# A fused forward and backward pass on one core: keeping grad_out and half of a large tensor on chip between the stages, recomputing a factor instead of spilling it, and spreading one stage's tiles between another's matmuls

## The chip, the cores and the metric

The kernel runs on one core of a Trainium2 chip. A core has a matrix engine (TensorE, PE in the profile), a vector engine (VectorE, DVE), an activation engine (ScalarE, ACT), a general-purpose engine (GpSimd, POOL) and a queueing engine (SyncE, SP), each with its own instruction stream, and 16 DMA engines that move data between memory, the on-chip SBUF and PSUM, where the matmuls accumulate. The metric is the device time in microseconds of one execution of the whole kernel; lower is better.

## The reference

Given x (2048 x 640), wqkv (640 x 1920), wo (640 x 640), w1 (640 x 1728), w2 (1728 x 640), a gate vector and grad_out (2048 x 640), all bfloat16, the kernel computes the output of a gated mix of linear attention and a two-layer network, and the gradients of that output with respect to x, wqkv, wo, w1, w2 and the gate (seven outputs):

```python
qkv = (x @ wqkv).reshape(B, S, 3, H, Dh)             # H = 32 heads of Dh = 20
phi = lambda t: where(t > 0, t + 1, exp(t)) + 1e-6
pq, pk = phi(q), phi(k)
kv  = einsum("bhsd,bhse->bhde", pk, v);  z = einsum("bhsd->bhd", pk)
o   = einsum("bhqd,bhde->bhqe", pq, kv) / (einsum("bhqd,bhd->bhq", pq, z)[..., None] + 1e-6)
a   = o.reshape(B, S, D) @ wo
b   = relu(x @ w1) @ w2
g   = sigmoid((x * gate_w).sum(-1, keepdims=True))
out = g * a + (1 - g) * b
_, vjp = jax.vjp(f, x, wqkv, wo, w1, w2, gate_w);  grads = vjp(grad_out)
```

## The kernel before

The 2048 rows are cut into NT = 16 tiles of 128 rows. D = 640 gives KD = 5 column blocks, F = 1728 gives KF = 14 (the last one half filled). Groups of G = 4 row tiles share a buffer in several places. Everything is bfloat16 but the sums in PSUM and a few per-row vectors.

The stages, in order: the k stage (x transposed, pk = phi(k)); Y = x^T pk; the forward loop; dw2; X; the backward network stage with small matrix products between its tiles; dk and dw1; dwk and dwq; dx.

**Forward loop** (lines 558 to 573). For each row tile, `q_main` computes q and pq = phi(q) (name pq, tiles tb). `q_post` sums pq times z per head, adds 1e-6, multiplies by 1 + exp(-logit), and takes the reciprocal: grd, one number per row and head, the gate over the attention's denominator. GpSimd multiplies pq by it (L486): pqg. `load_T` sends pqg through a DMA transpose to pqT. Then the factor e = grd * min(pq - 1e-6, 1), the derivative of phi times grd, is made by one VectorE and one GpSimd operation (L490, L491). `q_store` writes each pair of tiles of pqg and of e to memory (pqg_d, e_d) and loads the pair's rows of grad_out into a ring do_r. `h_half` computes the hidden layer; `out_chunk`, two tiles later, the output from hT and pqT and the sum T_t of output times grad_out (L540).

**dw2 stage** (lines 616 to 656). PE's main work is hs^T times doX: 14 chunks w2p, each of 16 pairs of matmuls, one pair per row tile. doX is grad_out with H = 32 further columns; all of it is loaded in four pieces at the end of the forward loop (L573). Between the chunks stand the 16 r tiles. `r_main` multiplies doT (grad_out transposed, by DMA, one group of four tiles at a time) by MT into a PSUM tile rp, copies it to SBUF on ScalarE (L589), multiplies by pqg (L591), sums by head (L592), scales (L594), and has GpSimd make wz = z times the result (L596). `r_post` subtracts wz from rp (L604, which frees rp's PSUM buffer) and multiplies by e (L607) into dq_st, and `r_store` sends pairs of dq to memory. The subtraction of a tile is issued after the next tile's `r_main`. pqg comes back from memory in four loads, e in eight, three of them ahead. After chunks 2 to 12 one or two r tiles follow:

```python
while 1 < m and done < NT and done < (m - 1) * NT / (KF - 4):
    r_main(done)
    if done >= 1:
        r_post(done - 1)
```

After chunk 9 the four transposes of w2 (w2T) are issued on SP's queue.

**X stage** (L665): pqg^T times doX, five PSUM tiles xp. It ends with `load_T(KV2_s, KVT_d)`, whose result `small_0` (tiles dwo) uses two row tiles into the next stage, where XT, the transpose of X, and woT are loaded too.

**What sets the order.** The tile framework decides the order of the instructions on each engine's stream from the program order and from its own estimates, and puts in the waits. All PSUM tiles come from one pool of four buffers, used in turn. Nearly all of SBUF is one arena: the `_Arena` class is told each buffer's size and the time span in which it lives (model times T_FF, T_DW2 and so on), and places them so that buffers whose spans overlap don't share space; a buffer's first write waits until the earlier users of its space are done. Loads and transposes are issued by SP in stream order; most output stores by ScalarE.

Of the kernel before, what the change touches and what calls it, by code (L numbers as in the profile page):

```python
# [14 lines left out]
P = 128  # L15
H = 32
# [3 lines left out]
class _Arena:  # L20
# [9 lines left out]

    def plan(self, limit, trials=6000):
        import random
        rnd = random.Random(1)
        order = sorted(self.items.items(), key=lambda kv: -kv[1][0] * (kv[1][2] - kv[1][1]))
        best = self._plan_order(order)
        for _ in range(trials):
            if best <= limit:
                break
            new = order[:]
            for _ in range(rnd.choice((1, 1, 2, 3))):  # L40
                new.insert(rnd.randrange(len(new)), new.pop(rnd.randrange(len(new))))
            tot = self._plan_order(new)
            if tot <= best:
                best, order = tot, new
        return self._plan_order(order)

# [31 lines left out]
def kernel(  # L78
# [38 lines left out]
    TF = (T_DW2 - T_FF) / NT  # L117
    T_H = T_DW2 - 10
    ar.add("xN", NT * D * B2, 0, T_FF)
    for g in range(NG):  # L120
# [15 lines left out]
    ar.add("MT", KD * D * B2, T_FF, T_X)  # L136
    ring("pqst", 2 * D, 3, T_FF, T_DW2)
    ring("hTf", KF * P, 3, T_FF, T_DW2 + 10)
    ring("pqT", D, 4, T_FF, T_DW2 + 10)
    ring("est", 2 * D, 2, T_FF, T_DW2)  # L140
    ring("dor", 2 * D, 3, T_FF, T_DW2 + 10)
    ring("ost", 2 * D, 2, T_FF, T_DW2 + 15)
    ar.add("doX", NT * DX * B2, T_H, T_FB)
    ar.add("pqg", NT * D * B2, T_DW2 + 5, T_FB)
    for g in range(NG):
        ar.add(f"doT{g}", G * P * KD * B2, T_DW2 + 10 + 6 * g, T_FB + 12 + 30 * (g + 1))
    ring("er", 2 * D, 3, T_DW2 + 10, T_X)
    ring("dqst", 2 * D, 2, T_DW2 + 10, T_X)
# [76 lines left out]
    wqT_s, wkT_s = mat("wqT"), mat("wkT")  # L225
    pqgN = aview("pqg", NT * D, i=NT)
    doX = aview("doX", NT * DX, i=NT)
    dkg = [aview(f"dk{g}", G * D, i=G) for g in range(NG)]
# [15 lines left out]
    KVT_d = dram.tile([D, D], BF16, name="KVT_d")  # L244
    e_d = dram.tile([S, D], BF16, name="e_d")
    dq_d = dram.tile([S, D], BF16, name="dq_d")
# [228 lines left out]
    def q_post(i):  # L475
        pq, tz = pqs.pop(i)
        pr, ii = i // 2, i % 2
        grd = tmp("grd", 3, [P, H], FP32)
        nc.vector.tensor_reduce(grd[:], heads(tz[:]), AX.X, ALU.add)
        nc.vector.tensor_scalar(grd[:], grd[:], 1e-6, rg_t[:, i:i + 1], ALU.add, ALU.mult)  # L480
        nc.vector.reciprocal(grd[:], grd[:])
        if ii == 0:
            e_st[pr] = rnext("est").rearrange("p (i d) -> p i d", i=2)
            pq_st[pr] = rnext("pqst").rearrange("p (i d) -> p i d", i=2)
        pqg = pq_st[pr][:, ii, :]
        nc.gpsimd.tensor_tensor(heads(pqg), heads(pq[:]), hb(grd[:]), ALU.mult)  # L486
        pqTs[i] = rnext("pqT").rearrange("p (c s) -> p c s", s=P)
        load_T(pqTs[i], pqg)
        dph = tmp("tb", 8)
        nc.vector.tensor_scalar(dph[:], pq[:], -1e-6, 1.0, ALU.add, ALU.min)  # L490
        nc.gpsimd.tensor_tensor(heads(e_st[pr][:, ii, :]), heads(dph[:]), hb(grd[:]), ALU.mult)  # L491

    def q_store(pr):
        nc.sync.dma_start(rows2(pqg_d, pr), pq_st.pop(pr))
        nc.sync.dma_start(rows2(e_d, pr), e_st.pop(pr))
        do_r[pr] = rnext("dor").rearrange("p (i d) -> p i d", i=2)
        load_N(do_r[pr], do2[2 * pr * P:(2 * pr + 2) * P, :])

# [24 lines left out]
    def out_chunk(i):  # L523
        pr, ii = i // 2, i % 2
        hT, pqT = hTs.pop(i), pqTs.pop(i)
        if ii == 0:
            ops[i] = pp("op")
        op = ops.pop(i)
        for kf in range(KF - 1):
            mm_cols(op, hT[:, kf, :], lambda a, e: w2_s[:, kf, a:e], ii == 0 and kf == 0, False)  # L530
        for k in range(KD):
            mm_cols(op, pqT[:, k, :], lambda a, e: M_s[:, k, a:e], False, ii == 1 and k == KD - 1)
        if ii == 0:
            ops[i + 1] = pp("op")
            tail_pair(op, ops[i + 1], hT[:, KF - 1, :], hTs[i + 1][:, KF - 1, :], w2_s[:, KF - 1, :], True)
        if ii == 0:
            o_st[pr] = rnext("ost").rearrange("p (i d) -> p i d", i=2)
        nc.scalar.copy(o_st[pr][:, ii, :], flat(op)[:, 0:D])
        jk = tmp("tb", 8)
        nc.vector.scalar_tensor_tensor(jk[:], flat(op)[:, 0:D], 1.0, do_r[pr][:, ii, :], ALU.mult, ALU.mult,  # L540
                                       accum_out=T_t[:, i:i + 1])
        if ii == 1:
            nc.scalar.dma_start(rows2(o0, pr), o_st.pop(pr))
# [37 lines left out]

    rps = {}

    def r_main(i):
# [5 lines left out]
        t_ = tmp("tb", 8)  # L590
        nc.vector.tensor_tensor(t_[:], rb[:], pqgN[:, i, :], ALU.mult)  # L591
        nc.vector.tensor_reduce(u_all[:, i, :], heads(t_[:]), AX.X, ALU.add)  # L592
# [3 lines left out]
        nc.gpsimd.tensor_tensor(heads(wz[:]), heads(zb[:]), hb(w32[:]), ALU.mult)  # L596
        nc.scalar.copy(doX[:, i, D:DX], w32[:])
        rps[i] = rp, wz

    def r_post(i):  # L600
# [4 lines left out]
        if ii == 0:  # L605
            dq_st[pr] = rnext("dqst").rearrange("p (i d) -> p i d", i=2)
        nc.vector.tensor_tensor(dq_st[pr][:, ii, :], s_[:], e_r[pr][:, ii, :], ALU.mult)  # L607
        if ii == 1:
            e_r.pop(pr)
            if pr + 3 < NT // 2:  # L610
                e_load(pr + 3)

    def r_store(pr):
        nc.sync.dma_start(rows2(dq_d, pr), dq_st.pop(pr))
# [317 lines left out]
```

## Time and profile before

| what | value |
|---|---|
| time, median of 3 runs (lowest to highest) | 655.67 us (655.65 to 656.07) |
| the profiled execution: time / span in the trace | 655.64 us / 653.9 us |
| mean granted clock of TensorE | 0.995 |
| PE busy | 636.0 us (97%) |
| VectorE, ScalarE, GpSimd busy | 262.6, 150.8, 120.7 us |
| moved by DMA | 108.44 MB |
| forward loop's steady part, 80 to 220 us | PE busy 139.11 of 140 us |
| dw2 stage, 220 to 245, 245 to 275, 275 to 315 us | PE busy 21.56, 28.54, 39.69 us |

How to read the lines that follow. Times are in microseconds from the span's start. A line of the timeline gives start, duration, engine, source line, operation, written tile <- read tiles, the shape, and in brackets the idle time before it with what ended it. In a wait line the three numbers are the total, the count and the longest. A line of the windows gives the stretch and its length, the busy time of PE, weight loads, VectorE, ScalarE and GpSimd (instructions in brackets), the granted clock, the DMA engines' share and GB/s. "SPq" and "ACTq" are DMA issues on those engines' queues; "arena" is any buffer of the arena.

### The profile page before, as it was taken

To read this page: it belongs to the slowest core of one execution; us is meant where nothing else is said; L and a number is where in the kernel's file an instruction comes from. 1 tells how busy PE (TensorE), PEld (TensorE's weight loads), DVE (VectorE), ACT (ScalarE), POOL (GpSimd) and SP (SyncE) were. 2 spreads that over 40 slices of the span, in tenths; PEclk is the share of its full clock that TensorE was granted. 3 is DMA by queue.
4 is the path that set the end of the run, shared out by engine and by line. 5 is a ranking of instruction groups with operands and counts; after the bars stand their busy time and mean duration, and the time that the engine had idled before them with its cause. 6 is when DMAs were issued, how large, how long until landed. Compare 5 with 4: busy or idle time off the path is not lost.

```text
span 653.9 us, 10503 instructions
## 1 busy us (share of the span) xinstructions
PE 636.0 (97%) x4400; PEld 357.6 (55%) x4480; DVE 262.6 (40%) x518; ACT 150.8 (23%) x209; POOL 120.7 (18%) x111
## 2 busy tenths in 40 slices
PE   9979999999999979999999999999999999999998
PEld 5536555555555545555555555555555555555554
DVE  4994654555445206566126332221016320104442
ACT  4401322212222113232134343442110111110000
POOL 5840534333343103243001000000000000000000
PEclk9979999999999999999999999999999999999999
DMA  9991884765447899731759999794118449991111
GB/s 259 313 368 60 208 169 88 157 132 145 116 88 173 252 279 214 201 111 61 176 124 214 233 259 248 146 267 124 39 47 196 117 106 278 259 219 58 42 42 43
DMA packets 229209, 108.44 MB, mean 166 GB/s; under 512 B 181802, under 2 KB 228458, under 8 KB 229162
## 3 DMA queue, kind: packets, MB, share of 16 engines
q1 hardware_dynamic: 217194, 93.02, 61.5%
q10 hardware_dynamic: 11968, 14.75, 6.6%
q8 instruction: 35, 0.57, 0.4%
q14 instruction: 12, 0.10, 0.0%
HBM read 31.54 MB, written 30.97 MB: 96 GB/s over the span
## 4 chain that ended last, share of the span: by engine, by line
PE 87%; DVE 4%; SPq 3%; DMA 3%; issue 1%; ACT 1%; POOL 0%; DVEq 0%; ACTq 0%; POOLq 0%
SPq L307 3%; DMA arena<-in_grad_out_dram 2%; DVE arena L362 2%; PE yp_531 L317 1%; PE w1p_4639 L773 1%; PE w1p_4770 L773 1%; PE w1p_5090 L773 1%; PE w1p_4867 L773 1%; PE w1p_4571 L773 1%; PE w1p_5283 L773 1%; PE w1p_5226 L773 1%; PE w1p_5158 L773 1%; PE w1p_5021 L773 1%; PE w1p_4702 L773 1%; PE op_2315 L317 1%
## 5 line engine op out<-in xcount | busy, mean ns | idle before, releaser
L317 PEld LDWEIGHTS <-arena 128*128 128x128 bf16 x2818 | 219.0, 98 | 179.6 <-issue 11.0
L773 PEld LDWEIGHTS <-arena 128*128 128x128 bf16 x320 | 30.8, 98 | 26.9 <-issue 0.5
L686 PEld LDWEIGHTS <-arena 128*128 128x128 bf16 x320 | 30.5, 98 | 26.7 <-issue 1.3
L504 PEld LDWEIGHTS <-arena 128*128 128x128 bf16 x320 | 30.4, 98 | 25.8
L406 POOL TENSOR_TENSOR arena<-arena 128x640 f32<-128x640 f32 x14 | 20.1, 1434 | 4.8 <-DVE arena L362 4.0
L757 DVE TENSOR_TENSOR tb_4845<-dkp_4834,dzb 128x640 bf16<-128x640 f32 x1 | 0.8, 825 | 41.5 <-PE dkp_4834 L317 41.5
L669 PEld LDWEIGHTS <-arena 128*128 128x128 bf16 x80 | 7.8, 98 | 9.6 <-issue 0.3
L861 PEld LDWEIGHTS <-arena 128*128 128x128 bf16 x80 | 7.8, 98 | 9.5
L874 DVE SCALAR_TENSOR_TENSOR f_5688<-gwb,dl_t,arena 128x640 f32<-128x640 bf16 x1 | 0.9, 885 | 28.4 <-DMA arena<-dxB_d 28.4
L339 PEld LDWEIGHTS <-arena 128*128 128x128 bf16 x140 | 7.9, 97 | 2.1 <-issue 1.0
L317 PE MATMUL yp_489<-arena 128*128 128x512 bf16 (+1 forms) x32 | 4.9, 308 | 4.0 <-DVE arena L362 4.0
L722 POOL MEMSET arena<- 128x3200 bf16 x1 | 2.8, 2764 | 31.2 <-DMA arena<-arena 31.2
L862 PEld LDWEIGHTS <-arena 128*128 128x128 bf16 x80 | 7.8, 98 | 0.0
L670 PEld LDWEIGHTS <-arena 128*128 128x128 bf16 x80 | 7.8, 98 | 0.0
L591 DVE TENSOR_TENSOR tb_2492<-tb_2490,arena 128x640 bf16<-128x640 bf16 x1 | 0.5, 492 | 16.8 <-ACT tb_2490 L589 16.8
L317 PE MATMUL yp_531<-arena 128*128 128x128 bf16 (+1 forms) x31 | 6.6, 387 | 0.1
L773 PE MATMUL w1p_4639<-arena 128*128 128x432 bf16 x32 | 6.0, 346 | 0.0
L773 PE MATMUL w1p_4770<-arena 128*128 128x432 bf16 x32 | 6.0, 346 | 0.0
L773 PE MATMUL w1p_4571<-arena 128*128 128x432 bf16 x32 | 6.0, 346 | 0.0
L773 PE MATMUL w1p_4867<-arena 128*128 128x432 bf16 x32 | 6.0, 346 | 0.0
L773 PE MATMUL w1p_5090<-arena 128*128 128x432 bf16 x32 | 6.0, 346 | 0.0
L773 PE MATMUL w1p_5226<-arena 128*128 128x432 bf16 x32 | 6.0, 346 | 0.0
(1065 smaller groups left out, 1217.9 us busy)
## 6 DMA issues: line engine op xcount, KB each, us to landing
out_dram<-arena ACTq DMA_DIRECT2D x28, 160.0 KB, 3.6
pk_d<-arena SPq DMA_DIRECT2D x4, 640.0 KB, 9.5
arena<-in_grad_out_dram SPq DMA_DIRECT2D x8, 320.0 KB, 4.5
pqg_d<-arena SPq DMA_DIRECT2D x8, 320.0 KB, 5.7
e_d<-arena SPq DMA_DIRECT2D x8, 320.0 KB, 3.9
out_dram<-arena ACTq DMA_DIRECT2D x8, 320.0 KB, 2.6
arena<-pqg_d SPq DMA_DIRECT2D x4, 640.0 KB, 4.6
arena<-in_grad_out_dram SPq DMA_DIRECT2D x4, 640.0 KB, 7.9
```

The source lines that it names most:

```text
L307: nc.sync.dma_start_transpose(dst, src.rearrange("s (c p) -> s c p", p=P))
L317: nc.tensor.matmul(ps_tile[:, b, 0:e - a], lhsT=lhsT, rhs=rhs_fn(a, e), start=start, stop=stop, **kw)
L339: nc.tensor.matmul(ps_tile[:, bank, a - 512 * bank:e - 512 * bank], lhsT=lhsT_fn(j), rhs=rhs_mat[:, j, a:e], start=bank not in seen, stop= ...
L362: nc.vector.scalar_tensor_tensor(dst, ps_flat, 1.0 + 1e-6, cp[:], ALU.add, ALU.max)
L406: nc.gpsimd.tensor_tensor(zacc, zacc, pkN[:, i, :], ALU.add)
L504: nc.tensor.matmul(hp[:, nb, 0:NBW], lhsT=xT(i, k), rhs=w1_s[:, k, blk * NBW:(blk + 1) * NBW], start=(k == 0), stop=(k == KD - 1))
L669: nc.tensor.matmul(xp[:, 0, :], lhsT=lhsT, rhs=doX[:, i, 0:512], start=(i == 0), stop=(i == NT - 1))
L670: nc.tensor.matmul(xp[:, 1, 0:DX - 512], lhsT=lhsT, rhs=doX[:, i, 512:DX], start=(i == 0), stop=(i == NT - 1))
L686: nc.tensor.matmul(gp[:, nb, 0:NBW], lhsT=doTg[i // G][:, k, gsl(i)], rhs=w2T_s[:, k, blk * NBW:(blk + 1) * NBW], start=(k == 0), stop=(k ...
L773: nc.tensor.matmul(wp[:, nb, 0:NBW], lhsT=xN2[:, i, csl(m)], rhs=hs(i)[:, blk * NBW:(blk + 1) * NBW], start=(i == 0), stop=(i == NT - 1))
L861: nc.tensor.matmul(wp[:, 0, :], lhsT=lhsT, rhs=dqN[:, i, 0:512], start=(i == 0), stop=(i == NT - 1))
L862: nc.tensor.matmul(wp[:, 1, 0:D + 1 - 512], lhsT=lhsT, rhs=dqN[:, i, 512:D + 1], start=(i == 0), stop=(i == NT - 1))
```

## The change

grad_out: each group of four tiles of doX is loaded once, in the forward loop (before tiles 1, 5, 9 and 13), serves the sum T_t there, and stays until the X stage; the ring do_r and its eight loads go. pqg: groups 2 and 3 are written by GpSimd straight into the buffers that the later stages read; groups 0 and 1 are stored and reloaded as before (NSP = 2). e: it is no longer made, stored and reloaded; grd is kept for all tiles, and `e_prep` computes min(pqg - 1e-6 grd, grd), the same factor, in the dw2 stage, by one GpSimd and one VectorE operation per tile, in three buffers. The r tiles come when the count of matmul pairs reaches 24 + 11.5 k, also within a chunk. Since the arena's content changes, its plan is made anew, with a longer search.

```diff
...
     T_Y, T_FF, T_DW2, T_X, T_FB, T_DW1, T_DWK, T_DX, T_END = 26, 48, 190, 273, 296, 432, 512, 556, 640
     TF = (T_DW2 - T_FF) / NT
     T_H = T_DW2 - 10
+    NSP = 2
     ar.add("xN", NT * D * B2, 0, T_FF)
     for g in range(NG):
         ar.add(f"xT{g}", G * D * B2, 0, T_FF + 5 + (T_H - T_FF - 5) * (g + 1) / NG)
...
     ar.add("KVT", KD * D * B2, T_FF - 20, T_FF + 30)
     ar.add("M", KD * D * B2, T_FF, T_DW2 + 10)
     ar.add("MT", KD * D * B2, T_FF, T_X)
-    ring("pqst", 2 * D, 3, T_FF, T_DW2)
+    ring("pqst", 2 * D, 3, T_FF, T_FF + TF * G * NSP + 5)
     ring("hTf", KF * P, 3, T_FF, T_DW2 + 10)
     ring("pqT", D, 4, T_FF, T_DW2 + 10)
-    ring("est", 2 * D, 2, T_FF, T_DW2)
-    ring("dor", 2 * D, 3, T_FF, T_DW2 + 10)
+    ar.add("grd", NT * H * 4, T_FF - 10, T_X)
     ring("ost", 2 * D, 2, T_FF, T_DW2 + 15)
-    ar.add("doX", NT * DX * B2, T_H, T_FB)
-    ar.add("pqg", NT * D * B2, T_DW2 + 5, T_FB)
+    for g in range(NG):
+        ar.add(f"doX{g}", G * DX * B2, T_FF + TF * G * g, T_FB)
+        ar.add(f"pqg{g}", G * D * B2, T_FF + TF * G * g if g >= NSP else T_DW2 + 5, T_FB)
     for g in range(NG):
         ar.add(f"doT{g}", G * P * KD * B2, T_DW2 + 10 + 6 * g, T_FB + 12 + 30 * (g + 1))
-    ring("er", 2 * D, 3, T_DW2 + 10, T_X)
     ring("dqst", 2 * D, 2, T_DW2 + 10, T_X)
     ring("w2st", D, 4, T_DW2, T_X + 5)
     ar.add("w2T", KD * F * B2, T_X - 30, T_DW1)
...
     X_s, XT_s, woT_s, wvT_s, KV2_s = mat("X"), mat("XT"), mat("woT"), mat("wvT"), mat("KV2")
     dKV_s, dKVT_s, Q_s, N_s = mat("dKV"), mat("dKVT"), mat("Q"), mat("N")
     wqT_s, wkT_s = mat("wqT"), mat("wkT")
-    pqgN = aview("pqg", NT * D, i=NT)
-    doX = aview("doX", NT * DX, i=NT)
+    pqgg = [aview(f"pqg{g}", G * D, i=G) for g in range(NG)]
+    doXg = [aview(f"doX{g}", G * DX, i=G) for g in range(NG)]
+    grd_all = aview("grd", NT * H * 2).bitcast(FP32).rearrange("p (i h) -> p i h", i=NT)
     dkg = [aview(f"dk{g}", G * D, i=G) for g in range(NG)]
     dqN = aview("dq", NT * DQX, i=NT)
     dxB = aview("dxB", NT * D, i=NT)
...
     def hs(i):
         return hsg[i // G][:, i % G, :]
+    def pqg(i):
+        return pqgg[i // G][:, i % G, :]
+
+    def doX(i):
+        return doXg[i // G][:, i % G, :]
+
     def gsl(i):
         return slice((i % G) * P, (i % G + 1) * P)
...
     def q_post(i):
         pq, tz = pqs.pop(i)
         pr, ii = i // 2, i % 2
-        grd = tmp("grd", 3, [P, H], FP32)
-        nc.vector.tensor_reduce(grd[:], heads(tz[:]), AX.X, ALU.add)
-        nc.vector.tensor_scalar(grd[:], grd[:], 1e-6, rg_t[:, i:i + 1], ALU.add, ALU.mult)
-        nc.vector.reciprocal(grd[:], grd[:])
-        if ii == 0:
-            e_st[pr] = rnext("est").rearrange("p (i d) -> p i d", i=2)
-            pq_st[pr] = rnext("pqst").rearrange("p (i d) -> p i d", i=2)
-        pqg = pq_st[pr][:, ii, :]
-        nc.gpsimd.tensor_tensor(heads(pqg), heads(pq[:]), hb(grd[:]), ALU.mult)
+        grd = grd_all[:, i, :]
+        nc.vector.tensor_reduce(grd, heads(tz[:]), AX.X, ALU.add)
+        nc.vector.tensor_scalar(grd, grd, 1e-6, rg_t[:, i:i + 1], ALU.add, ALU.mult)
+        nc.vector.reciprocal(grd, grd)
+        if i < NSP * G:
+            if ii == 0:
+                pq_st[pr] = rnext("pqst").rearrange("p (i d) -> p i d", i=2)
+            pg = pq_st[pr][:, ii, :]
+        else:
+            pg = pqg(i)
+        nc.gpsimd.tensor_tensor(heads(pg), heads(pq[:]), hb(grd), ALU.mult)
         pqTs[i] = rnext("pqT").rearrange("p (c s) -> p c s", s=P)
-        load_T(pqTs[i], pqg)
-        dph = tmp("tb", 8)
-        nc.vector.tensor_scalar(dph[:], pq[:], -1e-6, 1.0, ALU.add, ALU.min)
-        nc.gpsimd.tensor_tensor(heads(e_st[pr][:, ii, :]), heads(dph[:]), hb(grd[:]), ALU.mult)
+        load_T(pqTs[i], pg)
     def q_store(pr):
-        nc.sync.dma_start(rows2(pqg_d, pr), pq_st.pop(pr))
-        nc.sync.dma_start(rows2(e_d, pr), e_st.pop(pr))
-        do_r[pr] = rnext("dor").rearrange("p (i d) -> p i d", i=2)
-        load_N(do_r[pr], do2[2 * pr * P:(2 * pr + 2) * P, :])
+        if pr in pq_st:
+            nc.sync.dma_start(rows2(pqg_d, pr), pq_st.pop(pr))
     def h_half(i, half):
         hp = pp("hp")
...
             o_st[pr] = rnext("ost").rearrange("p (i d) -> p i d", i=2)
         nc.scalar.copy(o_st[pr][:, ii, :], flat(op)[:, 0:D])
         jk = tmp("tb", 8)
-        nc.vector.scalar_tensor_tensor(jk[:], flat(op)[:, 0:D], 1.0, do_r[pr][:, ii, :], ALU.mult, ALU.mult,
+        nc.vector.scalar_tensor_tensor(jk[:], flat(op)[:, 0:D], 1.0, doX(i)[:, 0:D], ALU.mult, ALU.mult,
                                        accum_out=T_t[:, i:i + 1])
         if ii == 1:
             nc.scalar.dma_start(rows2(o0, pr), o_st.pop(pr))
...
     q_post(0)
     LAG = 2
     for i in range(1, NT + LAG):
+        if i < NT and i % G == 1:
+            g = i // G
+            load_N(doXg[g][:, :, 0:D], do2[g * G * P:(g + 1) * G * P, :])
         if i < NT:
             q_main(i)
             h_half(i, 0)
...
             out_chunk(i - LAG)
         if i < NT - 1 and i % 2 == 1:
             h_half(i, 1)
-        if i == NT - 1:
-            for g in range(NG):
-                load_N(doX[:, g * G:(g + 1) * G, 0:D], do2[g * G * P:(g + 1) * G * P, :])
-
-
-    e_r, dq_st = {}, {}
-
-    def e_load(pr):
-        e_r[pr] = rnext("er").rearrange("p (i d) -> p i d", i=2)
-        load_N(e_r[pr], e_d[2 * pr * P:(2 * pr + 2) * P, :])
+
+    dq_st = {}
     rps = {}
+
+    es = {}
+
+    def e_prep(i):
+
+        es[i] = tmp("e", 3)
+        nc.gpsimd.tensor_tensor(heads(es[i][:]), heads(pqg(i)), hb(grd6[:, i, :]), ALU.subtract)
+        nc.vector.tensor_tensor(heads(es[i][:]), heads(es[i][:]), hb(grd_all[:, i, :]), ALU.min)
     def r_main(i):
         rp = pp("rp")
...
         rb = tmp("tb", 8)
         nc.scalar.copy(rb[:], flat(rp)[:, 0:D])
         t_ = tmp("tb", 8)
-        nc.vector.tensor_tensor(t_[:], rb[:], pqgN[:, i, :], ALU.mult)
+        nc.vector.tensor_tensor(t_[:], rb[:], pqg(i), ALU.mult)
         nc.vector.tensor_reduce(u_all[:, i, :], heads(t_[:]), AX.X, ALU.add)
         w32 = tmp("grd", 3, [P, H], FP32)
         nc.vector.tensor_scalar(w32[:], u_all[:, i, :], rg_t[:, i:i + 1], None, ALU.mult)
         wz = tmp("f32", 3, dt=FP32)
         nc.gpsimd.tensor_tensor(heads(wz[:]), heads(zb[:]), hb(w32[:]), ALU.mult)
-        nc.scalar.copy(doX[:, i, D:DX], w32[:])
+        nc.scalar.copy(doX(i)[:, D:DX], w32[:])
         rps[i] = rp, wz
+        if i + 1 < NT:
+            e_prep(i + 1)
     def r_post(i):
         pr, ii = i // 2, i % 2
...
         nc.vector.tensor_tensor(s_[:], flat(rp)[:, 0:D], wz[:], ALU.subtract)
         if ii == 0:
             dq_st[pr] = rnext("dqst").rearrange("p (i d) -> p i d", i=2)
-        nc.vector.tensor_tensor(dq_st[pr][:, ii, :], s_[:], e_r[pr][:, ii, :], ALU.mult)
-        if ii == 1:
-            e_r.pop(pr)
-            if pr + 3 < NT // 2:
-                e_load(pr + 3)
+        nc.vector.tensor_tensor(dq_st[pr][:, ii, :], s_[:], es.pop(i)[:], ALU.mult)
     def r_store(pr):
         nc.sync.dma_start(rows2(dq_d, pr), dq_st.pop(pr))
-    e_load(0)
-    e_load(1)
-    e_load(2)
+    grd6 = u_all
+    nc.vector.tensor_scalar(grd6[:], grd_all, 1e-6, None, ALU.mult)
     for g in range(NG):
-        load_N(pqgN[:, g * G:(g + 1) * G, :], pqg_d[g * G * P:(g + 1) * G * P, :])
         load_T(doTg[g], do2[g * G * P:(g + 1) * G * P, :])
+        if g < NSP:
+            load_N(pqgg[g], pqg_d[g * G * P:(g + 1) * G * P, :])
+    e_prep(0)
+    R0, RSTEP = 24, 11.5
     done = 0
-    for m in range(KF):
-        wp = pp("w2p")
-        st = rnext("w2st")
-        if m < KF - 1:
-            for i in range(NT):
-                mm_cols(wp, hs(i)[:, csl(m)], lambda a, e: doX[:, i, a:e], i == 0, i == NT - 1)
-            nc.scalar.copy(st, flat(wp)[:, 0:D])
-            nc.scalar.dma_start(out_5[m * P:(m + 1) * P, :], st)
-        else:
-            for i in range(0, NT, 2):
-                for b, (a, e) in enumerate(DSPL):
-                    for t in range(2):
-                        nc.tensor.matmul(wp[t * FT:(t + 1) * FT, b, 0:e - a], lhsT=hs(i + t)[:, m * P:F],
-                                         rhs=doX[:, i + t, a:e], start=(i == 0), stop=(i == NT - 2),
-                                         skip_group_check=True)
-            w2e = tmp("f32", 3, dt=FP32)
-            w2o = tmp("f32", 3, dt=FP32)
-            nc.scalar.copy(w2e[:], flat(wp)[:, 0:D])
-            nc.scalar.dma_start(w2o[0:FT, :], w2e[FT:P, :])
-            nc.gpsimd.tensor_tensor(st[0:FT, :], w2e[0:FT, :], w2o[0:FT, :], ALU.add)
-            nc.scalar.dma_start(out_5[m * P:F, :], st[0:FT, :])
-        while 1 < m and done < NT and done < (m - 1) * NT / (KF - 4):
+
+    def r_due(step):
+        nonlocal done
+        if done < NT and step >= R0 + RSTEP * done:
             r_main(done)
             if done >= 1:
                 r_post(done - 1)
...
             done += 1
             if done == NT:
                 r_post(NT - 1)
+
+    for m in range(KF):
+        wp = pp("w2p")
+        st = rnext("w2st")
+        if m < KF - 1:
+            for i in range(NT):
+                r_due(m * NT + i)
+                mm_cols(wp, hs(i)[:, csl(m)], lambda a, e: doX(i)[:, a:e], i == 0, i == NT - 1)
+            nc.scalar.copy(st, flat(wp)[:, 0:D])
+            nc.scalar.dma_start(out_5[m * P:(m + 1) * P, :], st)
+        else:
+            for i in range(0, NT, 2):
+                for b, (a, e) in enumerate(DSPL):
+                    for t in range(2):
+                        nc.tensor.matmul(wp[t * FT:(t + 1) * FT, b, 0:e - a], lhsT=hs(i + t)[:, m * P:F],
+                                         rhs=doX(i + t)[:, a:e], start=(i == 0), stop=(i == NT - 2),
+                                         skip_group_check=True)
+            w2e = tmp("f32", 3, dt=FP32)
+            w2o = tmp("f32", 3, dt=FP32)
+            nc.scalar.copy(w2e[:], flat(wp)[:, 0:D])
+            nc.scalar.dma_start(w2o[0:FT, :], w2e[FT:P, :])
+            nc.gpsimd.tensor_tensor(st[0:FT, :], w2e[0:FT, :], w2o[0:FT, :], ALU.add)
+            nc.scalar.dma_start(out_5[m * P:F, :], st[0:FT, :])
         if m == KF - 5:
             for q_ in range(4):
                 load_T(w2T_s[:, :, q_ * 432:(q_ + 1) * 432], B_w2[q_ * 432:(q_ + 1) * 432, :])
...
```

More of the change, by code (lines that the diff above doesn't have):

```diff
@@ L29, in add, with plan @@
         self.items[name] = [nbytes, t0, t1, None]
-    def plan(self, limit, trials=6000):
+    def plan(self, limit, seeds=24, trials=3000):
         import random
[L33 to L45, printed above, removed]
+        start = sorted(self.items.items(), key=lambda kv: -kv[1][0] * (kv[1][2] - kv[1][1]))
+        found = (self._plan_order(start), start)
+        for seed in range(seeds):
+            rnd = random.Random(seed)
+            order, best = start, self._plan_order(start)
+            for _ in range(trials):
+                if found[0] <= limit:
+                    break
+                new = order[:]
+                for _ in range(rnd.choice((1, 1, 2, 3))):
+                    new.insert(rnd.randrange(len(new)), new.pop(rnd.randrange(len(new))))
+                tot = self._plan_order(new)
+                if tot <= best:
+                    best, order = tot, new
+                    if best < found[0]:
+                        found = (best, order)
+        return self._plan_order(found[1])
     def _plan_order(self, order):
@@ L244 @@
     KVT_d = dram.tile([D, D], BF16, name="KVT_d")
-    e_d = dram.tile([S, D], BF16, name="e_d")
     dq_d = dram.tile([S, D], BF16, name="dq_d")
@@ L458 @@
     nc.vector.tensor_scalar(omg_t[:], g_t[:], -1.0, 1.0, ALU.mult, ALU.add)
-    e_st, pq_st, do_r, pqTs, hTs, o_st = {}, {}, {}, {}, {}, {}
+    pq_st, pqTs, hTs, o_st = {}, {}, {}, {}
     pqs = {}
@@ L667 @@
         for i in range(NT):
-            lhsT = pqgN[:, i, csl(m)]
-            nc.tensor.matmul(xp[:, 0, :], lhsT=lhsT, rhs=doX[:, i, 0:512], start=(i == 0), stop=(i == NT - 1))
-            nc.tensor.matmul(xp[:, 1, 0:DX - 512], lhsT=lhsT, rhs=doX[:, i, 512:DX], start=(i == 0), stop=(i == NT - 1))
+            lhsT = pqg(i)[:, csl(m)]
+            nc.tensor.matmul(xp[:, 0, :], lhsT=lhsT, rhs=doX(i)[:, 0:512], start=(i == 0), stop=(i == NT - 1))
+            nc.tensor.matmul(xp[:, 1, 0:DX - 512], lhsT=lhsT, rhs=doX(i)[:, 512:DX], start=(i == 0), stop=(i == NT - 1))
         nc.scalar.copy(X_s[:, m, :], flat(xp)[:, 0:D])
```

## The prediction

> **What bounds the kernel now.** I read the page's first line and busy times, then PE's waits, then the windows by stage, then PE, SP, DVE and POOL along the dw2 stage (220 to 312 us), where nearly all of the change lies.
>
> ```profile
> span 653.9 us, 10503 instructions
> PE 636.0 (97%) x4400; PEld 357.6 (55%) x4480; DVE 262.6 (40%) x518; ACT 150.8 (23%) x209; POOL 120.7 (18%) x111
> ...
> PE rp_2479 L317 <- DMA arena<-in_grad_out_dram: 3.3, 1, 3.3
> PE w2p_2814 L317 <- DVE tb_2750 L604: 1.2, 1, 1.2
> PE mtp_816 L339 <- DVE arena L510: 0.2, 1, 0.2
> 80.00:220.00 140.00, 139.11 (x929) 76.41 (x946) 68.91 (x137) 31.57 (x40) 55.45 (x43) 1.00 0.62 137
> 220.00:245.00 25.00, 21.56 (x158) 11.95 (x160) 1.84 (x5) 3.69 (x6) 0.72 (x1) 1.00 1.10 290
> ```
>
> PE is busy 636.0 of 653.9 us, and the change leaves its matmuls as they are. After 60 us PE waits 4.7 us in all; the two large waits stand in dw2: 3.28 us for doT0 (first r tile) and 1.25 us for an r tile's subtraction. So at most 4.5 us can be won, and the question is what new waits the denser r loop makes. The profiled execution took 655.64 us (1.74 outside the span) against a median of 655.67; I sum on 655.64. A difference of 0.2%, 1.31 us, is about what a measurement of this kernel can tell from none.
>
> **What costs nothing.** In the forward loop 16 POOL multiplies (1.27 us each, 20 us), 16 DVE operations, and the stores and loads of e and of half pqg go. There PE is 139.11 of 140 us busy and waits for nobody: no gain. The doX loads come earlier, under a DMA share of 0.62. They would cost only if a load held up SP's queue in which pqT and hT stand; at one place it does: hT15's transpose, issued at about 216.0 behind doT1, is wanted at 221.4, and with a transpose's 5.4 to 5.7 us (the KVT one below took 5.4) it is 0 to 0.3 late; I take 0.1. The first three e tiles and the DVE operation for 1e-6 times grd fall into 220 to 245, where DVE is busy 1.84 of 25 us and PE has two dw2 chunks before r0: nothing. If pqg0 landed later than 231, they would delay the first r product; it is issued at 217.6 and such loads take 4.6 to 7.7.
>
> **The first r tile.** Today doT0's transpose is issued at 230.83, behind the e loads and pqg loads, and lands 12.3 us later; the other doT transposes take 6.1 to 6.6 us. After the change SP's order is hT14, doT1, pqT15, hT15, pqg0, pqg1, doT2, w2T0, doT0. w2T0 reuses space of w2 and waits for the last output tile's matmuls (225.2), its issue takes 2.8 to 3.3; doT0 then goes out at about 228.2. PE wants r0 after 24 matmul pairs: w2 begins at 226.72, a chunk of 16 pairs takes 4.35, a pair 0.272, so 233.24. Landing after 5.4 (the KVT transpose) to 6.6 gives 233.6 to 234.8, a wait of 0.3 to 1.6; I take 1.0 for the 3.28.
>
> **The 1.25 us wait.** It came from a dq store issued late behind four w2T transposes:
>
> ```profile
> 251.51 13.19 SPq L307 DMA_TRANSPOSE arena<-in_B_w_dram  x4
> ...
> 265.37 0.47 SPq L614 DMA_DIRECT2D dq_d<-arena  x1
> ...
> 269.80 0.49 DVE L607 TENSOR_TENSOR arena<-tb_2725,arena 128x640 bf16<-128x640 bf16 x1 [1.37 <-DMA dq_d<-arena]
> ```
>
> These transposes now precede the first dq store, so the wait goes: -1.25.
>
> **The r loop.** An r tile comes every 11.5 pairs: T = 11.5 x 0.272 + 1.36 = 4.48 us. Each now also needs a POOL subtract (L591 of the new file) and a DVE minimum (L592). By the instruction order of the new program, DVE does for tile i: product (L601), subtraction of tile i-1 (L616), reduction, dq product of i-1 (L619), scale (L604), minimum for tile i+2. POOL does the subtract for tile i+2, then wz(i) (L606). The subtract has to wait until L619 of i-1 frees one of three e buffers; wz(i), queued behind it, waits too; and the subtraction of tile i waits for wz(i). That closes a cycle from one L616 to the next:
>
> ```profile
> 252.97 0.82 DVE L604 TENSOR_TENSOR tb_2580<-rp_2500,f_2518 128x640 bf16<-128x640 f32 x1
> 253.71 0.81 DVE L592 TENSOR_REDUCE u_all<-tb_2572 128x32 f32<-128x640 bf16 x1
> 254.43 0.48 DVE L607 TENSOR_TENSOR arena<-tb_2580,arena 128x640 bf16<-128x640 bf16 x1
> ...
> 69.08 1.27 POOL L491 TENSOR_TENSOR arena<-tb_842,grd_836 128x640 bf16<-128x640 bf16 x1
> 255.21 1.38 POOL L596 TENSOR_TENSOR f_2577<-zb,grd_2575 128x640 f32<-128x640 bf16 x1 [4.04 <-DVE grd_2575 L594]
> ```
>
> From the starts: subtraction 0.74, reduction 0.72, dq product 0.48, hand-over 0.08; then POOL 1.25 (like L491) and 1.36 (L596), hand-over 0.06: C = 4.69. Single terms vary (POOL 1.23 to 1.38, hand-over 0.08 to 0.16): 4.54 to 4.83. That is without a collision of minimum and wz, which become ready at the same moment. The minimum reads two SBUF tensors. The nearest rows are L442's products, also with two SBUF inputs, beside POOL's adds:
>
> ```profile
> 36.21 2.00 DVE L442 SCALAR_TENSOR_TENSOR tb_523<-arena,gwb 128x640 bf16<-128x640 bf16 x1
> 38.88 0.81 DVE L442 SCALAR_TENSOR_TENSOR tb_525<-arena,gwb 128x640 bf16<-128x640 bf16 x1
> 39.62 2.01 DVE L442 SCALAR_TENSOR_TENSOR tb_527<-arena,gwb 128x640 bf16<-128x640 bf16 x1
> ...
> 36.07 1.46 POOL L406 TENSOR_TENSOR arena<-arena 128x640 f32<-128x640 f32 x1
> 39.10 1.84 POOL L406 TENSOR_TENSOR arena<-arena 128x640 f32<-128x640 f32 x1 [1.57 <-DVE arena L362]
> ```
>
> L442 takes 0.81 alone and 2.0 when it starts in a POOL add, ending 0.68 after the add's end (38.21 after 37.53); the add in turn takes 1.84 instead of 1.46 when a product runs before it. So I take it that the two don't overlap: the minimum ends 0.62 after wz, and the product of the next tile (0.41), which stands behind it on DVE, still comes before L616: C = 0.74 + 0.72 + 0.48 + 0.08 + 1.25 + 1.27 + 0.62 + 0.41 = 5.57; if the minimum goes first, up to 5.8; down to 5.5 with the shorter hand-overs. Ends for the cycle: 4.54 to 5.8, value 5.57, since L442 is the nearest row in operands.
>
> The Trainium skill speaks against this step ("SBUF — State Buffer", "Who interferes with whom"): a VectorE instruction with two SBUF inputs and a GpSimd instruction that reads SBUF exclude each other, and the second one blocks fully until the first has ended. L442 beside L406 agrees. By that rule the sum below is 666.6; by the undisturbed durations of the operations alone it would be 655.2.
>
> What PE pays: PSUM's four buffers go round, and r15 needs the buffer of r13, which L616 frees. Measured from r0's start, the first L616 stands behind the product of r1: r1 starts at 12 x 0.272 + 1.36 = 4.62, copy and product take 2.69 (rp_2559 at 250.28, L604 at 252.97), the subtraction 0.82, hand-over 0.06: 8.2. Unhindered, r15 starts at 173 x 0.272 + 15 x 1.36 = 67.3. So the loss is 13 C - 59.1: 1.9 us at 4.69, nothing at 4.55, 3.7 at 4.83, 13.3 at 5.57 (12.4 at 5.5, 16.3 at 5.8). It shows at r4, r5, r8, r11, r12 and r15, at up to 3.4 us each.
>
> **KV2.** Its transpose went first after the X stage:
>
> ```profile
> 330.94 3.18 SPq L307 DMA_TRANSPOSE arena<-KVT_d  x1
> 334.24 5.17 SPq L307 DMA_TRANSPOSE arena<-arena  x4
> 339.58 3.41 SPq L307 DMA_TRANSPOSE arena<-in_A_wo_dram  x1
> ...
> 345.97 0.52 PE L339 MATMUL dwo_3569<-arena 128*128 128x140 bf16 x7
> ```
>
> Its new place in SBUF lies over the last pqg group, which the X stage reads to its end, and the scheduler puts it behind four XT transposes and woT. XT0 at 332.8, 4 x 1.33, woT 3.46: issue at 341.6, and with its 5.4 us it lands at 347.0; PE wants it at 345.97. Cost 0.8 to 2.0, taken 1.1.
>
> **Sum.** 655.64 - 3.28 - 1.25 + 1.0 + 0.1 + 1.1 = 653.3 without the loop; with its 13.3: 666.6. Own range 664 to 670 (cycle 5.5 to 5.8, other terms by their bounds).
>
> **Rivals.**
> - The loop keeps up (faster). If subtract and wz take their shorter times and the minimum doesn't block, the cycle is at most 4.55 and the time 653.3. Below a cycle of 4.62 the kernel is faster by over 1.31 us. For it: POOL is busy 9.54 of 30 us in dw2 now, DVE 16.91. Against it: L442's rows.
> - The loop lags by POOL's serial work alone: 4.69, loss 1.9, time 655.2; within 0.2% from 4.62 to 4.83. That is the case of the minimum not being held off although L442 is; its output is written over its input and one operand is a broadcast, which no row shows.
> - doT0 lands as late as it does now, 12.3 us after its issue, because doT2 and w2T0 crowd the DMA engines (share 1.10 in 220 to 245): r0 waits 7.3 instead of 1.0, 6.3 us more: 672.9 with the blocked minimum, 661 without. Against it: some 4 MB of transfers around it are gone.
> - The change doing less than it says: no case, the order shows the e traffic gone.
>
> **Numbers.** Forecast 0.66; keeps up 0.13 (faster); lags by POOL alone 0.12 (same); doT0 late 0.09 (slower). So faster 0.13, same 0.12, slower 0.75. The range takes in forecast and the third case, 654.5 to 670.5, and leaves out the faster rival and most of the late doT0, 0.19.
>
> **What would show it.** L592 at about 1.9 instead of 0.8, ending some 0.6 after L606; L616 every 5.6 us; PE waits for L616 at r4 to r15 adding up to 13; r0 waiting 1 for grad_out; the first dwo matmul 1.1 for KVT; no wait behind a dq store. I am wrong if L592 stays at 0.8 beside a running L606, or L616 keeps to 4.5.

## The result, and the profile after

The changed kernel takes 672.23 us (median, 671.61 to 673.42) against 655.87 for the kernel before in the same comparison: 1.025 times as long, 95% interval 1.0232 to 1.0268. The profiled execution took 672.27 us, span 670.2. The forecast was slower, 666.6 us, with a range up to 670.5; the sign and the main cause held, the size did not.

The head of the page after, and PE's waits (total, count, longest):

```profile
span 670.2 us, 10459 instructions
PE 639.3 (95%) x4400; PEld 358.3 (53%) x4480; DVE 283.8 (42%) x519; ACT 150.4 (22%) x209; POOL 118.8 (18%) x111
```

```profile
PE rp_2340 L327 <- DMA arena<-in_grad_out_dram: 4.5, 1, 4.5
...
PE rp_2758 L327 <- DVE tb_2729 L616: 3.1, 1, 3.1
PE rp_3131 L327 <- DVE tb_3101 L616: 2.8, 1, 2.8
PE rp_2916 L327 <- DVE tb_2886 L616: 2.8, 1, 2.8
PE dwo_3523 L349 <- DMA arena<-KVT_d: 1.4, 1, 1.4
...
PE rp_2547 L327 <- DVE tb_2518 L616: 1.1, 1, 1.1
PE rp_2973 L327 <- DVE tb_2940 L616: 1.0, 1, 1.0
PE rp_2601 L327 <- DVE tb_2571 L616: 0.7, 1, 0.7
```

The six tiles that wait for L616 are r8, r15, r11, r4, r12 and r5, the six that were named, for 11.5 us together. The wait behind a dq store is gone. Two things are larger than forecast: the first r tile waits 4.5 us for grad_out, and PE is busy 639.3 us instead of 636.0 with the same matmuls. The windows show where the second comes from (the third number from the end is the granted clock):

```profile
225.00:229.80 4.80, 4.80 (x38) 2.67 (x36) 4.47 (x4) 0.69 (x1) 3.33 (x3) 1.00 0.83 170
236.50:239.30 2.80, 2.65 (x11) 1.28 (x12) 0.00 (x0) 0.00 (x0) 0.00 (x0) 0.50 0.95 190
239.30:242.40 3.10, 3.10 (x19) 1.60 (x18) 1.55 (x3) 0.91 (x2) 0.33 (x1) 0.70 0.88 184
242.40:245.00 2.60, 2.55 (x20) 1.46 (x20) 0.00 (x0) 0.69 (x1) 0.94 (x1) 1.00 0.91 188
...
320.50:324.80 4.30, 4.30 (x24) 2.15 (x22) 3.25 (x7) 0.69 (x1) 1.53 (x2) 0.70 0.21 76
```

After the idle 4.5 us the clock is 0.50, then 0.70: r0 takes 2.63 us instead of 1.36 and the eight pairs after it 3.10 instead of 2.17, a loss of 2.2. Behind r15's wait it falls again; r15 and eleven pairs take 6.1 instead of 4.35, a loss of 1.8. In the kernel before, the wait of 3.28 us left it at 1.00.

The r loop in the profile after, first VectorE, then GpSimd:

```profile
246.16 0.82 DVE L616 TENSOR_TENSOR tb_2415<-rp_2340,f_2358 128x640 bf16<-128x640 f32 x1
...
247.62 0.48 DVE L619 TENSOR_TENSOR arena<-tb_2415,e_2285 128x640 bf16<-128x640 bf16 x1
...
249.48 1.87 DVE L592 TENSOR_TENSOR e_2461<-e_2461,arena 128x640 bf16<-128x640 bf16 x1 [1.23 <-POOL e_2461 L591]
251.28 0.48 DVE L601 TENSOR_TENSOR tb_2453<-tb_2451,arena 128x640 bf16<-128x640 bf16 x1
251.68 0.81 DVE L616 TENSOR_TENSOR tb_2464<-rp_2391,f_2409 128x640 bf16<-128x640 f32 x1
```

```profile
248.18 1.27 POOL L591 TENSOR_TENSOR e_2461<-arena,u_all 128x640 bf16<-128x640 bf16 x1 [4.84 <-DVE arena L619]
249.41 1.27 POOL L606 TENSOR_TENSOR f_2409<-zb,grd_2407 128x640 f32<-128x640 bf16 x1
```

L619 frees the e buffer, GpSimd subtracts, then makes wz; the minimum starts with wz (249.48 against 249.41) and ends at 251.35, 0.67 after it; the product and L616 follow. From one L616 to the next it is 5.52 us. The minimum is not slow by itself: where GpSimd was idle, in the same kernel, it took 0.81 (the second line here; in the first, GpSimd ran a subtraction from 226.48 to 228.33).

```profile
227.12 1.89 DVE L592 TENSOR_TENSOR e_2361<-e_2361,arena 128x640 bf16<-128x640 bf16 x1
228.94 0.81 DVE L592 TENSOR_TENSOR e_2412<-e_2412,arena 128x640 bf16<-128x640 bf16 x1
```

### The profile page after: what moved, and what is told of

Same layout as the page of the kernel before. It is cut to its first block, busy times and chain, and to the rows that moved or that the text cites. A ratio compares the mean times of both kernels' runs of the same rounds, so it can differ in the third digit from the quotient of the medians.

```text
span 670.2 us, 10459 instructions
## 1 busy us (share of the span) xinstructions
PE 639.3 (95%) x4400; PEld 358.3 (53%) x4480; DVE 283.8 (42%) x519; ACT 150.4 (22%) x209; POOL 118.8 (18%) x111
## 4 chain that ended last, share of the span: by engine, by line
PE 76%; DVE 5%; issue 4%; POOL 2%; DMA 2%; ACT 0%; ACTq 0%
DVE u_all L602 1%; DMA arena<-in_grad_out_dram 1%; PE w1p_4593 L788 1%; PE w1p_4724 L788 1%; DMA arena<-KVT_d 1%; PE w1p_5180 L788 1%; PE w1p_4975 L788 1%; PE w1p_4525 L788 1%; PE w1p_5044 L788 1%; PE w1p_4821 L788 1%; PE w1p_4656 L788 1%; PE w1p_5237 L788 1%; PE w1p_5112 L788 1%; PE op_2230 L327 1%; DVE arena L619 1%
## 5 line engine op out<-in xcount | busy, mean ns | idle before, releaser
L327 PE MATMUL yp_488<-arena 128*128 128x512 bf16 (+1 forms) x32 | 4.7, 299 | 4.0 <-DVE arena L372 4.0
L327 PE MATMUL rp_2340<-arena 128*128 128x512 bf16 (+1 forms) x10 | 2.8, 472 | 4.5 <-DMA arena<-in_grad_out_dram 4.5
```

The costliest lines, as they stand in the source:

```text
L327: nc.tensor.matmul(ps_tile[:, b, 0:e - a], lhsT=lhsT, rhs=rhs_fn(a, e), start=start, stop=stop, **kw)
```

## The experiments

The theory: the recomputed e makes the loop late, because VectorE operations with two SBUF inputs and GpSimd operations run one after the other; the late first r tile and the clock behind it come on top. Rivals: GpSimd's two operations in series are enough; the dense spacing of the r tiles is what cannot be kept; the loop's pace swallows the first tile's wait.

**The e work.** First, L592 left out, so that e lacks the minimum everywhere:

```diff
-        nc.vector.tensor_tensor(heads(es[i][:]), heads(es[i][:]), hb(grd_all[:, i, :]), ALU.min)
```

> The changed kernel without the minimum of e (L592): e is pqg - 1e-6 grd everywhere. Theory (operations of VectorE with two SBUF inputs and GpSimd's operations exclude each other): the minimum's 1.87 us go, but the next product (two SBUF inputs) now collides with GpSimd: the cycle becomes about 5.0 us, loop waits about 5 to 6 instead of 11.5, time near 667. Rival (only GpSimd's two operations in series matter, the minimum is slow by itself): cycle 4.7, the product stays at 0.48, loop waits 2, time near 663.

One execution, 661.05 us; r waits for L615 (the subtraction) 3.3 us, for grad_out 4.1. The cycle is 4.84 to 4.90, between the two expectations. The time lies under both (667 and 663): with waits of at most 1.2 us in the loop the slow matmuls behind r15, 1.8 us in the changed kernel, are gone too, and neither had counted them. The rows show the exclusion still at work, now on the product:

```profile
254.18 1.21 DVE L600 TENSOR_TENSOR tb<-tb,arena 128x640 bf16<-128x640 bf16 x1 [1.62 <-ACT tb L598]
258.52 0.49 DVE L600 TENSOR_TENSOR tb<-tb,arena 128x640 bf16<-128x640 bf16 x1 [1.13 <-ACT tb L598]
```

```profile
253.77 1.27 POOL L605 TENSOR_TENSOR f<-zb,grd 128x640 f32<-128x640 bf16 x1
258.62 1.53 POOL L605 TENSOR_TENSOR f<-zb,grd 128x640 f32<-128x640 bf16 x1
```

In the first pair the product is held until wz is nearly done (it ends at 255.39, wz at 255.04; 0.7 us added); in the second the product comes first and wz is 0.26 longer.

Then the subtract of e moved to VectorE, so that GpSimd has only wz:

```diff
-        nc.gpsimd.tensor_tensor(heads(es[i][:]), heads(pqg(i)), hb(grd6[:, i, :]), ALU.subtract)
+        nc.vector.tensor_tensor(heads(es[i][:]), heads(pqg(i)), hb(grd6[:, i, :]), ALU.subtract)
```

> The changed kernel with the subtract of e on VectorE instead of GpSimd: GpSimd has only wz in the loop, VectorE 4.0 us of own work per tile. Exclusion theory: wz (1.27) overlaps none of subtract, minimum and product, so the cycle is 4.0 + 1.27 = 5.2 us, some rows of L591, L592 or L601 are longer by up to 1.2 us, and the loop waits about 8 us: near 669. Rival (the queue on GpSimd makes the cycle): 4.5 us, no loop waits, about 661.

664.76 us, 1.0121 (1.0096 to 1.0145). The cycle is 4.95, not 4.5 as the rival wants: with GpSimd's queue out of the way the loop is still late, by 4.2 us of waits instead of 11.5.

```profile
252.64 0.81 DVE L591 TENSOR_TENSOR e<-arena,u_all 128x640 bf16<-128x640 bf16 x1
253.49 1.78 DVE L592 TENSOR_TENSOR e<-e,arena 128x640 bf16<-128x640 bf16 x1
```

```profile
252.87 1.72 POOL L606 TENSOR_TENSOR f<-zb,grd 128x640 f32<-128x640 bf16 x1 [3.24 <-DVE grd L604]
```

wz is held 0.45 by the subtract, then holds the minimum, which ends 0.68 after it: three operations in line. The expectation was 0.25 too long for the cycle and 4 us too long for the time.

Last, the part undone: e is made in the forward loop, stored, and reloaded in pairs, as in the kernel before; the rest stays changed.

```diff
+        nc.vector.tensor_scalar(dph[:], pq[:], -1e-6, 1.0, ALU.add, ALU.min)
...
+        nc.gpsimd.tensor_tensor(heads(ef[i][:]), heads(dph[:]), hb(grd), ALU.mult)
...
+            nc.sync.dma_start(e_d[j * P:(j + 1) * P, :], ef.pop(j)[:])
...
-        nc.gpsimd.tensor_tensor(heads(es[i][:]), heads(pqg(i)), hb(grd6[:, i, :]), ALU.subtract)
-        nc.vector.tensor_tensor(heads(es[i][:]), heads(es[i][:]), hb(grd_all[:, i, :]), ALU.min)
...
+            load_N(es[i // 2], e_d[i * P:(i + 2) * P, :])
```

> The changed kernel with one part undone: e is made in the forward loop, stored and reloaded (ring of four pairs); order of the r tiles and places in SBUF as in the changed kernel. Theory: all of the r loop's waits (11.5 us) go, since they come from the e work on GpSimd and VectorE; the first r tile waits as long as there or some 3 us longer, as two e loads go out ahead of doT0, with the lowered clock behind it: 661 to 664. Rival: the dense spacing of the r tiles itself makes the loop late; then half of its waits stay: 667 or more.

658.76 us, 1.0031 (1.0014 to 1.0047); span 657.3, 12.9 less than the changed kernel's. PE's waits in this run:

```profile
PE rp L333 <- DMA arena<-in_grad_out_dram: 4.8, 1, 4.8
PE yp L333 <- DVE arena L378: 4.0, 1, 4.0
PE warm L392 <- DVE arena L382: 1.3, 1, 1.3
PE dwo L355 <- DMA arena<-KVT_d: 1.2, 1, 1.2
```

No r tile waits for a subtraction any more, at the same spacing: the spacing alone does not make the loop late, the e work at this spacing does. No run has the e work at the old spacing. With the waits went r15's clock loss of 1.8 us, which the expectation had not counted; that is most of the 2 us by which the time lies under 661. The wait for doT0 was 0.3 us longer than in the changed kernel.

**The first r tile.** The r tiles of group 1 first, whose doT1 has landed long before:

```diff
+    seq = [4, 5, 6, 7, 0, 1, 2, 3] + list(range(8, NT))
...
-            r_main(done)
+            r_main(seq[done])
```

> The changed kernel, with the r tiles taken in another order: group 1 (tiles 4 to 7) first, then group 0, 2, 3. doT1 has landed long before r0 is due, so PE does not stop for grad_out. Theory: the wait of 4.5 us, and the lowered clock behind it (10 + 16 matmuls that took 2.2 us too long), are lost time that adds to the loop's, so the time falls by 6.7 us to about 665.5, with the r loop's waits as before (11 to 12 us, a subtraction every 5.5 us). Rival: the loop's pace absorbs an earlier start, or the clock drops at another place instead: then less than 3 us are won, 669 or more.

665.01 us, 1.013 (1.0102 to 1.0159); the span falls by 6.6 to 663.6. The wait for grad_out is gone, and what was won at r0 was not swallowed: r1 starts 4.7 us earlier than in the changed kernel, and so does r15. That the 6.6 come so near the expected 6.7 is in part luck. A new wait of 1.9 us stands before the first r tile, so that its start is only 2.5 us earlier (2.2 more are the clock there); the other 1.8 are r15's clock loss, which did not come this time, although its wait was 2.81 us again. Instead the clock fell to 0.66 in 275 to 280, behind r8's wait; these 1.5 us were swallowed, as the loop's waits fell from 11.5 to 10.1.

```profile
PE rp L327 <- DVE tb L616: 10.1, 6, 3.1
...
PE rp L327 <- DVE tb L547: 1.9, 1, 1.9
```

L547 is the last output tiles' sum, which frees a PSUM buffer and stands on VectorE behind the first three minimums, which wait for pqg1 here and run from 228.90 to 233.3. The prediction put these at nothing; in the changed kernel, where they needed pqg0 and ran from 225.3 to 229.7, that held.

The other side: the kernel before, with the spread of the r tiles alone.

```diff
-        while 1 < m and done < NT and done < (m - 1) * NT / (KF - 4):
...
+        if done < NT and step >= 24 + 11.5 * done:
```

> The kernel before with one part of the change alone: r tiles due every 11.5 matmul pairs from pair 24 on, everything else (e, pqg and doX from memory) as before. Theory: the spread needs doT0 at 233, and in the old traffic it lands at about 243, so TensorE stands 9 to 10 us instead of 3.3 and then runs at a lowered clock for some 2.5 us more; the r loop itself keeps up, since it has no e work. 664 to 668. Rival: the spread is what lets the r loop run without waits, and a late doT0 costs no more than it did: 652 to 656.

661.74 us, 1.0059 (1.0038 to 1.008).

```profile
PE rp L317 <- DMA arena<-in_grad_out_dram: 9.6, 1, 9.6
```

```profile
240.00:245.00 5.00, 2.93 (x11) 1.42 (x12) 0.00 (x0) 0.05 (x1) 0.00 (x0) 0.50 1.12 227
```

In the old traffic doT0 lands at 242, PE stands 9.6 us and comes back at half clock; no r tile waits for VectorE. The wait was as expected; the time came out 2 us below, and the dq store's wait of 1.25 us, which is gone here too, is a part of that. So the spread needs an early doT. In the changed kernel r0 starts 5.4 us earlier than here, and in e_spilled_alone, where e is still stored and reloaded, 4.0 us earlier; so most of this comes with the rest of the change, which keeps grad_out and half of pqg on chip. It was not early enough.

**The clock.** Five idle times of TensorE in each of two runs (one execution each), made by chains of VectorE copies between chunks of the dwk and dwq products of the kernel before:

```diff
+            nc.vector.tensor_copy(dm[:], flat(pv)[:, 0:D])
+            for _ in range(KS[m]):
+                nc.vector.tensor_copy(dm[:], dm[:])
+            nc.vector.tensor_copy(db[:], dm[:])
+            nc.tensor.matmul(wp[:, 0, :], lhsT=db[:, 0:P], rhs=db[:, 0:512], start=True, stop=True)
```

> The kernel before with five idle times of TensorE of growing length in the dwk and dwq products (a chain of VectorE copies between two chunks, then one extra matmul that reads its result). It asks from which idle time on the granted clock falls. If the clock falls after an idle time of more than about 3.5 us only, the gaps of 2 to 3 us leave it at 1.00, and each longer one costs 2 to 3 us of slow matmuls. Rival: shorter gaps lower it now and then, as the last r tile of the changed kernel suggests (2.8 us of idle time, clock 0.7 to 0.8 behind it).

> As gapA, with other lengths in another order, partly longer. The same expectation: gaps of over 3.5 us lower the clock behind them, shorter ones do not; the rival expects drops behind some of the gaps of 2.5 to 3.5 us too.

The 4.4 us after idle times of 2.70, 3.23, 3.76 and 4.35 us, in gapA:

```profile
551.10:555.50 4.40, 4.40 (x32) 2.50 (x33) 0.00 (x0) 0.00 (x0) 0.00 (x0) 1.00 1.13 231
563.40:567.80 4.40, 4.40 (x20) 2.18 (x21) 0.00 (x0) 0.00 (x0) 0.00 (x0) 0.64 1.10 257
577.80:582.20 4.40, 4.40 (x16) 2.07 (x17) 0.00 (x0) 0.00 (x0) 0.00 (x0) 0.50 1.04 239
594.10:598.50 4.40, 4.40 (x20) 2.18 (x21) 0.00 (x0) 0.00 (x0) 0.00 (x0) 0.64 0.02 4
```

All gaps from 3.23 us on lowered the clock (also 6.75 in gapA, and 3.29, 3.76, 4.81, 5.87 and 8.33 in gapB), the one of 2.70 did not. So the limit of 3.5 us in the expectation was wrong, and its rival right. The loss does not grow with the gap: the next 64 matmuls took 8.86 us after 2.70, 10.23 after 3.23, 10.26 after 4.81 and 11.56 after 3.76, so 1.4 to 2.7 us are lost; the 32 that are left after 6.75 lost 1.2. Nor does the length alone decide whether the clock falls. The wait of 3.28 us in the kernel before cost nothing. r8 waits 3.08 us in the changed kernel and in g1first; behind it the clock stayed at 1.00 in the first and fell in the second:

```profile
280.00:285.00 5.00, 4.82 (x35) 2.74 (x36) 3.77 (x7) 0.91 (x2) 2.50 (x2) 1.00 0.01 3
```

```profile
275.00:280.00 5.00, 4.60 (x23) 2.34 (x23) 3.77 (x6) 0.91 (x2) 2.50 (x2) 0.66 0.00 0
```

Of three waits of 2.81 us (r11 and r15 in the changed kernel, r15 in g1first) only r15's in the changed kernel lowered it. And the kernel before stands on this edge: in both gap kernels its own first r tile waits 3.7 us, and two r tiles then take 5.4 to 5.5 us instead of 2.7, at a clock of 0.50. Its executions in the comparisons took 653.7 to 658.4 us, the shortest at a mean clock of 0.997, the longest at 0.989. The Trainium skill ("TensorE: Matmul & The Clock Gate", "What's actually happening") gives the clock's monitor windows of about 3.4 us that run freely, with the drop after an idle one. That agrees with losses that don't follow the gap's length; the drops behind 2.81, 3.08, 3.23 and 3.29 us, all shorter than such a window, it does not explain.

**A version that keeps what is good.** best1 took the changed kernel with spilled e, group 1 first, KV2 placed over buffers that are free before the X stage ends (KV2 and dKVT to 169600, woT to 142464), and dq stored by ScalarE:

```diff
+    ar.items["KV2"][3] = 169600
+    ar.items["dKVT"][3] = 169600
+    ar.items["woT"][3] = 142464
...
-        nc.sync.dma_start(rows2(dq_d, pr), dq_st.pop(pr))
+        nc.scalar.dma_start(rows2(dq_d, pr), dq_st.pop(pr))
```

> The changed kernel with e made in the forward loop, stored and reloaded as in the kernel before (ring of four pairs), r tiles from group 1 on, dq stored by ScalarE's queue, and KV2 in a place that is free before the X stage ends. Theory: the r loop has no e work left and keeps up (cycle under 4 us), r0 does not wait, KV2 is in time: all waits after 60 us together under 1 us, time 655.6 - 4.5 = about 651. Rival: e loads or dq stores come late and take 2 us or more back: 653 or more.

653.26 us, 0.9955 (0.9934 to 0.9975), 2 us above the theory. Its e reloads ran ahead of their use, so some dq tiles got other rows' e. One chunk waited 2.2 us for a subtraction: ScalarE had no work from 236.95 to 242.58 and then issued an output store, with the copy of the next r tile behind it; what held the store, the trace does not show. espill mends the reloads (each after the pair that it replaces, as in e_spilled_alone) and gives the dq stores back to SyncE; espill_act leaves them on ScalarE.

> As best1, but each reload of e waits until the dq product of the pair whose place it takes is done (in best1 it did not, so the dq tiles were multiplied by e rows of other tiles; only its time is read), and dq is stored by SyncE again. Theory: the r loop needs no e work, r0 does not wait, KV2 is in time; PE waits after 60 us under 2 us, time about 651 to 653, faster than before. Rival: the dq stores stand behind four w2T transposes and the e reloads on SyncE's queue, the two dq buffers fill up, and the subtractions come late: 2 to 5 us of waits for them, 654 to 657.

> As espill, with dq stored from ScalarE's queue. Theory: no dq buffer waits, time about 651. Rival: a store on ScalarE's queue holds up the copies of rp and of the chunks behind it, as in best1 where the matmuls waited 2.2 us: 653 or more.

espill: 650.72 us, 0.9921 (0.9904 to 0.9937); espill_act: 650.73 us, 0.9912 (0.9895 to 0.9929). Both are faster than both kernels (than the kernel before by 0.8 to 0.9%), and where dq is stored makes no difference. espill_act differs from best1 only in the place of the reloads, and best1's wait of 2.2 us is not in it. PE's last wait in espill is at the start of the forward loop, and the dw2 stage has none:

```profile
PE kp L336 <- DVE arena L381: 0.6, 1, 0.6
PE mtp L358 <- DVE arena L533: 0.2, 1, 0.2
```

```profile
215.00:250.00 35.00, 35.00 (x261) 19.59 (x260) 9.81 (x23) 7.38 (x13) 5.13 (x5) 1.00 1.08 227
250.00:285.00 35.00, 35.00 (x260) 19.76 (x259) 19.58 (x40) 10.85 (x22) 10.16 (x8) 1.00 0.50 142
285.00:320.00 35.00, 35.00 (x270) 19.95 (x268) 16.15 (x35) 8.89 (x17) 7.88 (x6) 1.00 0.39 103
```

The gain is of the size of the two dw2 waits of the kernel before, 4.5 us, which the prediction named as the most that could be won: 5.2 us by the ratio, 3.5 by the two profiled spans; the profiled execution of before had no clock loss at its first r tile, which the two gap kernels, the same code up to there, had.

## Why the prediction was right in kind and wrong in size

- **The r loop (right).** Cycle 5.57 forecast, 5.52 measured; loss 13.3 forecast, 11.5 measured in the six named tiles. The rows of L442 beside L406 were the right ones: the minimum ended 0.67 after wz, as L442 ended 0.68 after the add. The wait lines start at the end of the matmul before, and that is 0.16 us after the next tile would have started in a row (1.52 in the rows against 1.36 from start to start); from start to start the six delays are 12.5 us. That is what 13 cycles of 5.52 give, since the two effects of the slow r0 nearly cancel: the first L616 ended 10.3 us after r0's start instead of 8.2, and PE itself was 2.2 later. One slip of the sum, 67.3 where its terms give 67.4, is 0.1 us.
- **The first r tile (the step that failed first).** "I take 1.0", measured 4.49. The bounds were 0.3 to 1.6, and three of its terms moved the same way. doT0 went out at 229.58, not 228.2: SyncE's queue was held by doT2's transpose, which took 7.5 us to issue, and w2T0's 3.4:

```profile
218.47 7.50 SPq L317 DMA_TRANSPOSE arena<-in_grad_out_dram  x1
226.07 3.40 SPq L317 DMA_TRANSPOSE arena<-in_B_w_dram  x1
229.58 3.69 SPq L317 DMA_TRANSPOSE arena<-in_grad_out_dram  x1
```

  It landed 7.0 us later, where about 6.0 had been taken from 5.4 to 6.6. And PE was there 1.1 us earlier than in the execution that the sum was made on; that lengthens the wait, not the time. The rival "doT0 lands late" (12.3 us, 7.3 of waiting) overstated it. The trace of before had shown such a hold: doT0's own issue took 7.38 of its 12.3 us. It went into no bound. The other doT transposes there landed 5.3 to 6.8 us after their issue, not 6.1 to 6.6 as the prediction has it.
- **The clock (left out, the second step that failed).** No term of the sum had it, and no reason was given. The trace of before showed an idle 3.28 us without a drop, and the forecast wait for doT0 was short; but the loop's predicted waits of 3.4 us were as long as gaps that lowered the clock in the gap kernels (3.23, 3.29), and a wait that does so has a price beyond its length. It was 2.2 us behind the first r tile and 1.8 behind r15; that r15's wait would lower it and r8's longer one not, no row could tell.
- **KV2, the dq store, the forward loop (right).** 1.1 forecast, 1.4 measured; the store's wait gone; no new wait in 80 to 220. hT15 was not late, for the 0.1 taken.
- **Sum.** r0 started at 236.65 instead of 234.3 (233.24 + 1.0 + 0.1), 2.3 later; 2.3 + 4.0 (clock) + 0.3 (KV2) - 0.8 (loop) = 5.8 over the forecast; 5.7 was measured. Either of the first two alone would have left the time inside the range; together they put it 1.7 us outside. The range was also drawn narrower than its terms: their upper bounds add up to 671.3, not to 670.

## What to carry to other kernels

Removing a transfer that is hidden wins nothing, and what replaces it must fit the engines of the stage into which it moves: count it as a cycle, buffer by buffer and queue by queue, with a VectorE operation that has two SBUF inputs and a GpSimd operation in line, not side by side. A range for a wait must take its worst neighbour in the trace as well as its usual one, and a wait of TensorE of about 3 us may carry some 2 us of slow matmuls behind it; every one of 3.7 us or more in the dw2 stages and the gap kernels here did. Before a stage is made denser, ask what its first tile needs and what stands ahead of that on the loading queue: here, the order of the groups alone brought the first r tiles 4.7 us forward.

## What the runs showed of the hardware that was not expected

- A TensorE wait of 3.2 us or more was followed in all nine such gaps of the two gap kernels by a clock of 0.50 to 0.68 over some 4 us, a loss of 1.2 to 2.7 us that does not grow with the length. Waits of 2.81 and 3.08 us lowered it in one kernel and left it at 1.00 in another place or kernel.
- One DMA transpose can hold SyncE's queue for 7.4 to 9.4 us at issue (doT0 in the kernel before, doT2 in the changed kernel and in g1first) where the other transposes of grad_out in these runs take 2.6 to 4.8.
- Where a GpSimd operation and a VectorE operation with two SBUF inputs met, the one that started first kept its usual time in the rows shown and the other was longer: the minimum ended 0.67 us after wz, and wz took 0.26 to 0.45 longer behind a product or a subtraction.
